# A new written order of steps for a fused attention and gated-FFN kernel, with eight reloaded weight chunks in place of six in block 2

## The chip, the cores and the metric

The kernel runs on one core of a Trainium2 chip. The metric is the device time of one execution in microseconds. The kernel before takes 946.95 us (median of 3 runs, 946.5 to 949.25).

## The reference

Linear attention over 8 batches, 8 heads, 576 positions and 64 values per head, then an RMS-normed, gated feed-forward network over the 4608 tokens that come out of it (model width 512, inner width 1536):

```python
q_s = np.exp(q - np.max(q, axis=-1, keepdims=True))
q_s = q_s / (np.sum(q_s, axis=-1, keepdims=True) + 1e-09)
k_s = np.exp(k - np.max(k, axis=2, keepdims=True))
k_s = k_s / (np.sum(k_s, axis=2, keepdims=True) + 1e-09)
kv = np.einsum('bhsd,bhse->bhde', k_s, v)
x = np.einsum('bhsd,bhde->bhse', q_s, kv)          # then reshaped to (4608, 512)
xn = x / np.sqrt(np.mean(x * x, axis=-1, keepdims=True) + 1e-06) * rms_g
g = xn @ w_gate
out = (g * (1.0 / (1.0 + np.exp(-g))) * (xn @ w_val)) @ w_out
```

Queries are softmaxed along the 64 values of a head, keys along the 576 positions; that is why the keys of a head group need a maximum over all positions before anything else can be done with them.

## The kernel before

**Tiling.** The 4608 tokens are nine blocks of 512. Blocks 0, 1 and 2 are computed plainly; the other six are taken as three pairs, whose two-block products are Strassen products (steps `pp` and, in the last two pairs, `qq` in place of the plain second product `f2p`). The inner width 1536 is twelve chunks of 128. A step number s = 12·j + i stands for chunk i of plain block j, so s = 0 to 11 is block 0, 12 to 23 block 1, 24 to 35 block 2. fp32 matmuls are three passes over halves in fp32r: each operand is split into a high half, a cast of it, and a low half, the operand less its high half.

**One chunk.** `f1.s.0` and `f1.s.1` (L964 to L974) are the gate and the value product of chunk s, twelve matmuls of 128x512 each, into one of only two PSUM banks of the pool `ps_gv`. `g_mul.s` (L977 to L979, DVE) reads the gate bank, `silu.s` (L982, ACT) works on the copy, and `h_mul.s` (L985, DVE) reads the value bank. So `f1.s+1.1`, which reuses the value bank, can't start ahead of the end of `h_mul.s`. `h_hi.s` and `h_lo.s` (L988 to L995) split the result, and `f2.s` (L998 to L1011) adds its product with the output weights to four banks, one chunk behind.

**Weights of a chunk.** Blocks 0 to 2 need gate, value and output weights of the chunk as halves. Each is either made anew on the engines from the weights held in SBUF (`w_hi`, L893, on ACT; `w_lo`, L896 to L898; `o_hi`, L901; `o_lo`, L904 to L906), or read back from the DRAM copy that `w_keep` and `o_keep` (L916 to L921, on SP's DMA queue) stored in block 1. `w_back` (L924 to L926, 1 MB) and `o_back` (L928 to L930, 512 KB) read back, issued from POOL. Both kinds of tile come from the pool `wsp` with two buffers, so that the halves of chunk s can be written only when chunk s−2 has been used for the last time. Before, chunks 24 to 29 make their halves and 30 to 35 read them back.

**Attention.** It is done by head groups, `b.n` being group n of batch b. `k_load` (L491 to L502, SP) brings the keys in, `k_max` (L533 to L535, DVE) takes the maximum of the parts, `k_tr` (L547 to L550, PE) transposes, `k_top` (L553, DVE) takes the maximum over positions, `k_rows` (PE), `k_sub` (DVE) and `k_exp` (ACT, table Exp) follow, then `k_mm` (L572 to L578, PE) makes the keys' product with the values. The steps `q_...` do the queries, ending with `q_x` (PE). A name with a 0 behind it, such as `k_max0`, is the form of it used for the first batch or batches. `warm` (L468 to L471) is a pair or a run of matmuls on a constant, whose result isn't used. `exp_table` (L473 to L476) is a small activation with Exp.

**What sets the order.** There is no planner in the kernel. One string, `ORDER` (lines 22 to 342, 3345 steps), lists the steps; each engine runs its own instructions in the order of the string, and DMAs go out in the order of the engine that issues them: loads, keeps and output stores on SP, reloads on POOL. A suffix puts a step on an engine (`:A` ACT, `:D` DVE, `:P` POOL):

```python
with tc.manual_schedule():
    for step in ORDER.split():
        step, _, engine = step.partition(":")
        name, *args = step.split(".")
        unit[0] = where[engine]
        steps[name](*map(int, args))
```

Of the kernel before, what the change touches and what calls it, by code (L numbers as in the profile page):

```python
# [27 lines left out]
q_eps0.0.1 k_top.0.2 q_exp.0.0 q_eps0.0.2 k_sub.0.1 v_load.0.2 k_tr.0.3 warm.2.13 conv_mul.0.1 k_rows.0.2 q_rec0.0.1  # L28
conv_low.0.1.1 q_rec0.0.2 warm.2.10 q_mul0.0.1:P k_sub.0.2 warm.2.3 k_exp.0.1 conv_shift.0.1 kv_zero.6 k_exp.0.2
q_t0.0.1 v_load.0.3 v_ones.1.0 q_mul0.0.2:P warm.2.12 k_top.0.3 k_eps.0.0 q_max0.0.3 conv_low.0.0.1 k_rows.0.3 warm.2.6  # L30
conv_add.0.1.1 k_rec.0.0 conv_mul.0.0 k_sub.0.3 q_t0.0.2 q_c0.0.1:A warm.2.4 g_load conv_shift.1.1 kv_norm0.0.0:A
k_mm.0.2 q_sub0.0.3:P load_w.0.2 k_exp.0.3 conv_shift.0.0 k_mm.0.1 k_load.1.0 k_eps.0.2 q_c0.0.2:A conv_add.0.0.1
# [5 lines left out]
conv_low.1.0.2 q_sub0.1.0:P load_w.1.2 q_x0.0.3 load_w.3.1 k_sub.1.0 load_w.2.1 n_sum0.1 x_hi.0.3:A o_hi.0:D x_lo.0.1
load_w.2.2 o_lo.0:P x_sq.0.3 n_sum0.2 v_load.1.0 conv_mul.1.0 x_lo.0.3 n_sum0.3 q_exp.1.0 conv_shift.1.0 warm.2.7
conv_add.1.0.2 conv_mul.2.0 n_t.0 warm.2.1 k_exp.1.0 f1.0.0.0.0 n_y0.0 f1.0.0.0.1 f1.0.0.0.2 q_max0.1.1 f1.0.0.0.3  # L40
f1.0.1.0.0 f1.0.0.1.0 conv_shift.2.0 load_w.4.0 f1.0.1.0.1 f1.0.1.0.2 q_sub0.1.1:P load_w.3.2 w_hi.1.0.2:A f1.0.1.0.3
n_y1.0 f1.0.0.1.1 load_w.3.0 f1.0.0.1.2 f1.0.0.1.3 q_load0.1.2 f1.0.1.1.0 q_exp.1.1 w_lo.1.1:P f1.0.1.1.1 f1.0.1.1.2
# [10 lines left out]
conv_add.3.2.1 conv_mul.5.1 f1.3.1 conv_mul.4.2 load_w.7.1 v_load.1.1 o_hi.2:A w_lo.3.0:P conv_shift.4.2 conv_low.5.0.2
o_lo.2:D conv_mul.5.0 f1.3.0 conv_add.4.0.2 conv_shift.5.1 o_hi.3:A conv_shift.5.0 h_hi.2:A conv_mul.6.1 q_sum0.1.2
load_w.7.2 load_w.6.2 q_eps0.1.2 w_hi.4.0.2:A load_w.8.1 h_lo.2:D k_tr.1.1 f2.2 load_w.8.0 g_mul.3 conv_low.4.2.1
w_lo.4.0:P k_top.1.1 q_rec0.1.2 silu.3 conv_shift.6.1 q_max.2.0 conv_add.5.0.2 k_rows.1.1 f1.4.0 conv_mul.5.2 k_sub.1.1
conv_low.5.2.1 h_mul.3 conv_mul.7.0 w_lo.4.1:P conv_shift.5.2 conv_low.6.0.2 f1.4.1 o_lo.3:P h_hi.3:A g_mul.4 k_max.1.2
silu.4 conv_add.4.2.1 k_exp.1.1 conv_shift.7.0 h_lo.3:P load_w.8.2 q_t0.1.1 load_w.10.1 k_tr.1.2 f2.3 q_c0.1.1:D
load_w.10.0 kv_zero.2 k_top.1.2 conv_add.5.2.1 conv_mul.7.1 q_half.2.0 w_hi.5.0.2:A conv_shift.7.1 kv_zero.5
load_w.10.2 o_hi.4:A w_lo.5.0:D v_load.1.2 k_mm.1.1 conv_low.7.0.2 o_lo.4:P k_rows.1.2 k_eps.1.1 f1.5.0 k_sub.1.2  # L60
q_max2.2.0 h_mul.4 q_sub.2.0:P q_max0.1.3 h_hi.4:A k_rec.1.1 conv_low.6.2.1 w_lo.5.1:D f1.5.1 q_exp.2.0 q_sub0.1.3:P
kv_norm0.1.1:D k_exp.1.2 g_mul.5 conv_add.6.0.2 q_sum.2.0 conv_mul.6.2 kv_hi.1.1:A q_half2.2.0 conv_low.7.2.1
conv_shift.6.2 q_x0.1.1 q_exp.1.3 h_lo.4:D f2.4 w_hi.6.0.2:A conv_add.7.0.2 x_hi.1.1:D x_sq.1.1 x_lo.1.1 silu.5
k_mm.1.2 w_lo.6.0:D load_w.9.1 conv_mul.8.0 f1.6.0 load_w.9.0 conv_add.6.2.1 k_eps.1.2 k_rec.1.2 o_hi.5:A q_sum0.1.3
h_mul.5 o_lo.5:P conv_shift.8.0 h_hi.5:A o_hi.6:A w_lo.6.1:D f1.6.1 conv_mul.8.1 g_mul.6 x_acc.1.1:P kv_norm0.1.2:A
w_hi.7.0.2:A kv_zero.3 q_eps0.1.3 h_lo.5:D conv_mul.8.2 w_lo.7.0:P q_rec0.1.3 conv_shift.8.1 f2.5 silu.6 q_sum2.2.0
conv_mul.7.2 o_lo.6:D conv_low.8.2.1 h_mul.6 q_mul0.1.2:P conv_shift.7.2 f1.7.0 q_rec.2.0 conv_add.7.2.1 conv_mul.9.1
conv_shift.8.2 kv_hi.1.2:A conv_low.8.0.2 w_lo.7.1:D v_ones.1.3 v_ones.2.1 load_w.9.2 v_load.2.1 conv_shift.9.1
conv_add.8.2.1 conv_low.10.2.1 q_t0.1.2 f1.7.1 q_c0.1.2:A conv_add.8.0.2 conv_mul.9.0 h_hi.6:A conv_shift.9.0
conv_low.9.0.2 g_mul.7 q_x0.1.2 h_lo.6:D silu.7 load_w.11.0 load_w.11.1 w_hi.8.0.2:A conv_add.9.0.2 f2.6 k_load.2.0  # L70
x_hi.1.2:D conv_mul.9.2 h_mul.7 x_sq.1.2 x_lo.1.2 o_hi.7:A load_w.11.2 conv_low.9.2.1 w_lo.8.0:D k_load.1.3 h_hi.7:A
f1.8.0 conv_shift.9.2 conv_mul.10.2 o_lo.7:D q_load.2.1 w_hi.9.0.2:A w_lo.8.1:D h_lo.7:D conv_mul.11.0 w_lo.9.1:P
# [1355 lines left out]
```

## Time and profile before

| what | value |
| --- | --- |
| median of 3 runs | 946.95 us (946.5 to 949.25) |
| the profiled execution | 947.29 us, its span 945.5 us |
| busy share of the span: PE, PEld, DVE, ACT, POOL | 98%, 79%, 77%, 50%, 57% |
| matmuls in the trace | 4625 |
| DMA | 211.79 MB, mean 224 GB/s |

PE is TensorE's matmuls, PEld its weight loads, DVE is VectorE, ACT ScalarE, POOL GpSimd, SP SyncE. Times in views are microseconds from the start of the span; L974 is line 974 of the kernel. A row of instructions has start, duration, engine, line, operation, tiles (written and read) and shapes; brackets hold the idle time ahead of it and what ended that. Four stretches help to find one's way: the first `f1` starts at 35.17, block 1's end lies near 268, the first paired product near 407, and the last matmul ends at 938.80.

### The profile page before, as it was taken

How to read it: one execution, taken by the hardware profiler on the slowest of the kernel's cores; microseconds unless marked ns; L12 is line 12 of the kernel's file. 1: busy time of each engine (PE TensorE's matmuls, PEld its weight loads, DVE VectorE, ACT ScalarE, POOL GpSimd, SP SyncE). 2: the span in 40 equal slices, each digit the busy share in tenths (PEclk: the TensorE clock that was granted, in tenths of full speed). 3: DMA queues.
4: the chain of work that ended last, by engine and by line, in shares of the span. 5: the costliest groups of instructions: out<-in, count | busy, mean ns of one | idle time of the engine just before them, and what ended most of it. 6: DMA issues, size and time to landing. Idle time of an engine off the chain costs nothing.

```text
span 945.5 us, 14391 instructions
## 1 busy us (share of the span) xinstructions
PE 922.8 (98%) x4625; PEld 747.9 (79%) x4625; DVE 728.3 (77%) x1522; ACT 468.9 (50%) x746; POOL 539.4 (57%) x531
## 2 busy tenths in 40 slices
...
GB/s 255 291 253 190 150 71 238 299 262 271 319 259 153 242 242 280 216 219 228 264 202 261 234 295 196 308 288 269 163 203 212 193 210 265 267 215 199 54 134 90
DMA packets 215463, 211.79 MB, mean 224 GB/s; under 512 B 139828, under 2 KB 176732, under 8 KB 210780
## 3 DMA queue, kind: packets, MB, share of 16 engines
...
## 4 chain that ended last, share of the span: by engine, by line
PE 78%; DMA 9%; DVE 6%; SPq 3%; ACT 1%; issue 1%; POOL 1%; DVEq 0%; POOLq 0%; ACTq 0%
PE ps_gv L1123 17%; PE ps_o L1123 12%; PE ps_gv L974 11%; PE ps_a L1123 7%; PE ps_o L1011 7%; PE ps_o L1332 6%; PE ps_o L1216 3%; PE ps_a L1332 3%; DMA qt<-in_q_dram 3%; PE ps_gv L1332 3%; PE ps_a L1216 2%; PE ps_gv L1216 2%; DMA kt<-in_k_dram 2%; PE ps_a L578 2%; DMA w<-in_moe_w_gate_dram 1%; PE ps_a L786 1%
## 5 line engine op out<-in xcount | busy, mean ns | idle before, releaser
L974 PE MATMUL ps_gv<-xh,w 128*128 128x512 f32 x576 | 190.3, 398 | 3.7 <-DVE gs L986 2.9
L1123 PE MATMUL ps_gv<-x,ring 128*128 128x512 f32 x576 | 143.0, 392 | 0.0
L974 PEld LDWEIGHTS ps_gv<-xh,w 128*128 128x128 f32 x576 | 108.8, 189 | 28.6 <-DVE gs L986 4.1
L1123 PEld LDWEIGHTS ps_gv<-x,ring 128*128 128x128 f32 x576 | 106.9, 188 | 22.3
L974 PE MATMUL ps_gv<-xl,w 128*128 128x512 f32 x288 | 112.5, 394 | 0.0
L1144 DVE TENSOR_TENSOR tmp<-tmp,ps_gv 128x512 f32<-128x512 f32 x84 | 57.2, 683 | 47.8 <-PE ps_gv L1123 46.2
L1123 PE MATMUL ps_o<-x,ring 128*128 128x512 f32 x360 | 85.0, 389 | 0.0
L1096 POOL DMA_DIRECT2D ring<-wd x54 | 30.9, 572 | 88.9 <-PE ps_gv L1123 39.8
L1123 PEld LDWEIGHTS ps_o<-x,ring 128*128 128x128 f32 x360 | 67.5, 188 | 14.3
L1011 PE MATMUL ps_o<-o,hh 128*128 128x512 f32 x288 | 74.3, 399 | 0.0
L974 PEld LDWEIGHTS ps_gv<-xl,w 128*128 128x128 f32 x288 | 54.7, 190 | 10.6 <-issue 0.2
L1011 PEld LDWEIGHTS ps_o<-o,hh 128*128 128x128 f32 x288 | 52.9, 188 | 12.2 <-issue 0.7
L409 ACT CAST hh<-gs 128x512 fp32r<-128x512 f32 x51 | 31.5, 617 | 49.4 <-POOL gs L1288 19.7
L898 POOL TENSOR_TENSOR w<-w,w 128x512 fp32r<-128x512 f32 x34 | 46.4, 1371 | 11.0 <-ACT w L409 4.3
L1144 DVE TENSOR_TENSOR tmp<-tmp,ps_o 128x512 f32<-128x512 f32 x42 | 28.7, 684 | 24.3 <-PE ps_o L1123 23.9
L535 DVE TENSOR_REDUCE cm<-kt 116x128 f32<-116x640 f32 x28 | 36.6, 1311 | 5.1 <-DMA kt<-in_k_dram 5.0
L1011 PE MATMUL ps_o<-o,hl 128*128 128x512 f32 x144 | 38.8, 391 | 0.9 <-DVE hl L995 0.9
L995 POOL TENSOR_TENSOR hl<-gs,hh 128x512 fp32r<-128x512 f32 x21 | 28.8, 1373 | 16.1 <-ACT hh L409 14.3
L1123 PE MATMUL ps_a<-x,ring 128*128 128x512 f32 x144 | 37.0, 392 | 0.0
L1123 PE MATMUL ps_a<-x,w 128*128 128x512 f32 x144 | 36.7, 390 | 0.0
L1096 POOL DMA_DIRECT2D w<-wd x18 | 10.2, 564 | 45.3 <-PE ps_a L1123 37.0
L1123 PE MATMUL ps_gv<-x,w 128*128 128x512 f32 x144 | 35.2, 392 | 0.0
...
## 6 DMA issues: line engine op xcount, KB each, us to landing
...
```

The source lines that it names most:

```text
L409: (e.copy if e is nc.scalar else e.tensor_copy)(dst, src)
L535: nc.vector.tensor_reduce(out=cm, in_=kt_[b, g].rearrange("p h j d -> p h d j"), axis=AX.X, op=ALU.max)
L578: nc.tensor.matmul(pk[h * D:(h + 1) * D, :D + 1], lhsT=ke[:n, h, j], rhs=vt[:n, j, h], start=(j == 0), stop=(j == len(rows) - 1))
L898: on(nc.gpsimd).tensor_tensor(out=w[:, :, 1], in0=halves(s % NF, a, 1)[:, 0], in1=w[:, :, 0].bitcast(F32), op=ALU.subtract)
L974: nc.tensor.matmul(pd[s], lhsT=w[:, a, c // 2, m, c % 2 * P:c % 2 * P + P], rhs=X[j, c][x], start=(n == 1), stop=(n == 3 * NKT))
L995: on(nc.gpsimd).tensor_tensor(out=hl, in0=g_[s], in1=h_[s][0].bitcast(F32), op=ALU.subtract)
L1011: nc.tensor.matmul(po[t], lhsT=a[:, t * P:(t + 1) * P], rhs=w, start=(i == 0 and n == 0), stop=(i == NF - 1 and n == len(terms) - 1))
L1096: nc.gpsimd.dma_start(t, src.rearrange("p a b f -> p (a b f)"))
L1123: nc.tensor.matmul(abc[p, i, m, b], lhsT=src[:, h, c * P:(c + 1) * P], rhs=operand(o, c, x), start=first and n == 0, stop=n == 5, skip_gro ...
L1144: nc.vector.tensor_tensor(out=dst, in0=ux[u + (src,)], in1=abc[u + (b,)], op=ALU.add)
L1216: nc.tensor.matmul(pa[p, t, k], lhsT=a[:, k * P:(k + 1) * P], rhs=w, start=(c == 0 and n == 0), stop=(c == NF - 1 and n == 2))
L1332: nc.tensor.matmul(qacc[p, b, x], lhsT=ws[l][x], rhs=h[m], start=first and i == 0 and n == 0, stop=i == NH - 1 and n == 2, skip_group_chec ...
```

## The change

Only the string `ORDER` changes; no function does. It has 3339 steps in place of 3345.

- Block 2 reads back chunks 28 to 35 in place of 30 to 35. Gone are `w_hi`, both `w_lo`, `o_hi` and `o_lo` of chunks 28 and 29; new are `w_back.28`, `w_back.29`, `o_back.28` and `o_back.29`. The DRAM copies they read are stored in block 1 as before.
- The first stage, up to the first `f1`, has another order: head groups of batch 0 finish in the order 0, 1, 3, 2; four `warm` pairs in place of two stand ahead of `k_tr.0.0`; `warm.2.9` moves there from the end of block 1; `exp_table` moves behind `silu.1`.
- The rest of blocks 0 to 2 has another order. PE's own steps change places mostly by a few positions, the small steps of DVE, ACT and POOL and the loads on SP by more. Some engine suffixes change (113 from DVE to POOL, 108 from POOL to DVE, 61 from ACT to DVE, 39 from DVE to ACT).
- From the second pair on PE's order is nearly the same. In the end two stores (`qput.2.11.1`) go behind those of `qput.2.21.1`.

The core of the diff, lines of the string:

```diff
@@ -20,325 +20,323 @@
 ORDER = """
-k_load.0.0 k_load.0.1 kv_zero.0 kv_zero.4 k_load.0.2 constants v_ones.0.3 q_load0.0.1 kv_zero.1 warm.2.11 v_ones.0.2
-v_ones.1.2 v_ones.0.1 v_ones.0.0 kv_zero0.0 q_load0.0.2 warm.2.8 k_max0.0.0 kv_zero0.1 k_load.0.3 k_max0.0.1 k_tr.0.0
-q_load0.0.0 warm.2.5 k_max0.0.2 warm.2.0 load_w.1.1 load_w.0.1 k_tr.0.1 v_load.0.0 k_top.0.0 q_max0.0.1 k_rows.0.0
-warm.9 q_max0.0.2 q_sub0.0.1:P k_sub.0.0 q_load0.0.3 q_sub0.0.2:P q_exp.0.1 q_max0.0.0 k_max0.0.3 load_w.0.0 v_load.0.1
-q_exp.0.2 q_sub0.0.0:P k_top.0.1 q_sum0.0.1 k_tr.0.2 k_exp.0.0 k_rows.0.1 warm.2.2 q_sum0.0.2 conv_mul.1.1 k_mm.0.0
...
-k_rec.0.2 q_sum0.0.0 q_exp.0.3 k_eps.0.1 kv_norm0.0.2:A k_rec.0.1 q_eps0.0.0 load_w.1.0 w_hi.0.0.2:A q_rec0.0.0
...
-q_mul0.1.0:P conv_mul.3.0 q_max0.1.2 w_hi.2.0.2:A load_w.5.0 h_lo.0:P conv_shift.3.0 q_t0.1.0 load_w.4.2 f2.0
-conv_mul.4.1 q_load.2.0 q_eps0.1.1 o_hi.1:A w_lo.2.1:P q_c0.1.0:D conv_low.3.0.2 g_mul.1 o_lo.1:D kv_hi.1.0:A
-conv_low.2.2.1 q_sub0.1.2:P conv_shift.4.1 q_x0.1.0 q_rec0.1.1 conv_mul.3.1 kv_zero.7 w_lo.2.0:D f1.2.0 conv_low.3.2.1
-v_ones.1.1 conv_shift.3.1 q_mul0.1.1:P silu.1 x_hi.1.0:A h_mul.1 conv_add.3.0.2 conv_mul.2.2 x_lo.1.0 x_sq.1.0 f1.2.1
-g_mul.2 conv_mul.3.2 conv_shift.2.2 h_hi.1:A load_w.5.2 w_hi.3.0.2:A h_lo.1:D load_w.7.0 conv_add.2.2.1 conv_shift.3.2
...
-h_hi.8:A conv_add.10.0.2 conv_mul.11.1 q_t0.1.3 f1.9.0 q_c0.1.3:D k_max.1.3 q_load.2.2 w_hi.10.0.2:A h_lo.8:D
-w_lo.10.1:P k_tr.1.3 f1.9.1 o_lo.8:D conv_add.9.2.1 k_top.1.3 g_mul.9 silu.9 k_rows.1.3 w_lo.10.0:D f1.10.0
...
-q_half.2.2 v_ones.2.0 v_load.2.0 q_load.2.3 w_lo.11.0:D f1.11.0 w_lo.11.1:P x_lo.1.3 x_acc.1.3:D q_max2.2.1 o_hi.11:D
...
-w_keep.22 q_load.4.0 q_lo.3.1:D o_lo.21:D q_x.3.0 h_mul.21 f1.22.0 s_add.4.1:D h_hi.21:A s_add.3.3:D w_hi.23.0.2:A
-h_lo.21:P s_hi.4.1:A o_hi.22:A q_sub.3.3:P q_x.3.1 g_mul.22 f1.22.1 k_max.3.3 o_lo.22:P silu.22 s_keep.1.3 x_sq.3.1
-o_keep.21 k_max.4.0 x_sq.3.0 s_hi.3.3:A q_exp.3.3 q_rec.3.2 w_lo.23.0:D f2.21 s_lo.4.1:D x_acc.3.1:D s_keep.4.1
-w_hi.24.0.2:A s_add.3.4:D v_load.3.3 w_lo.23.1:D s_hi.3.4:A f1.23.0 q_sum.3.3 s_add.5.3:P o_hi.23:A h_mul.22
...
-h_hi.25:A f1.26.1 g_mul.26 o_lo.25:P kv_hi.4.0:A k_max.4.1 silu.26 h_lo.25:P q_sum2.4.1 q_rec.4.1 kv_lo.4.0 k_load.4.2
...
-k_max.4.2 silu.27 k_load.4.3 v_ones.4.3 s_lo.4.4:P q_half2.4.2 v_load.4.3 n_lo.3:P k_eps.4.1 k_rec.4.1 q_t.4.1
-kv_hi.4.1:A f2.26 w_lo.28.0:P h_mul.27 x_sq.4.0 kv_lo.4.1 q_hi.4.1:A s_lo.5.4:D o_hi.27:A h_hi.27:A q_sum2.4.2
...
-n_t.3 q_mul.4.2:P q_exp.4.3 h_lo.27:D q_lo.4.1:P n_y0.3 s_hi.5.3:A k_rows.4.2 f1.28.1 k_sub.4.2 s_keep.4.4 o_lo.27:P
-q_t.4.2 r_keep.3 k_exp.4.2 q_sum.4.3 q_load.5.0 w_lo.29.0:P q_half2.4.3 q_x.4.1 g_mul.28 w_back.30 f2.27 x_sq.4.1
-k_max.4.3 s_lo.5.3:P x_cp.4.1:A silu.28 n_y1.3 w_lo.29.1:P s_keep.5.3 k_tr.4.3 f1.29.0 q_sum2.4.3 q_rec.4.3 h_mul.28
...
-x_nm.3.1:D v_ones.5.0 x_nm.3.3:D b_hi.0.0.1:A o_in.0.0.0 k_rec.4.3 v_load.5.0 k_max.5.0 b_lo.0.0.1:P kv_hi.4.3:A
...
-qb_lo.2.4.3:D qput.2.11.1 qpua.2.11.1 qb_hi.2.4.4:A qb_hi.2.4.5:D qput.2.22.1 qq.2.4.3 qb_hi.2.3.0:A qb_lo.2.4.4:D
...
-qb_lo.2.3.4:D qput.2.21.0 qpua.2.21.0 qb_hi.2.3.5:D qput.2.21.1 qpua.2.21.1 qq.2.3.3 qb_lo.2.3.5:P qq.2.3.4.0
...
+k_load.0.0 k_load.0.1 kv_zero0.0 k_load.0.2 constants v_ones.0.0 q_load0.0.1 v_ones.1.1 warm.2.1 v_ones.0.3 v_ones.0.2
+kv_zero.4 kv_zero.5 v_ones.0.1 q_load0.0.2 kv_zero0.1 warm.2.2 k_max0.0.0 k_load.0.3 warm.2.8 q_load0.0.0 warm.2.3
+load_w.1.1 load_w.0.1 k_tr.0.0 warm.2.10 k_top.0.0 v_load.0.0 k_max0.0.1 k_rows.0.0 warm.2.6 q_max0.0.1 k_tr.0.1
+q_load0.0.3 k_sub.0.0 q_sub0.0.1:P load_w.0.0 k_exp.0.0 kv_zero.1 k_max0.0.2 v_load.0.1 k_top.0.1 k_tr.0.2 k_max0.0.3
+q_exp.0.1 q_sum0.0.1 k_tr.0.3 v_load.0.2 warm.2.13 k_top.0.2 q_max0.0.0 k_rows.0.1 conv_low.0.1.1 q_eps0.0.1 k_top.0.3
...
+f1.0.0.2.3 f1.0.1.2.0 w_lo.1.0:P conv_mul.1.2 f1.0.1.2.1 conv_shift.2.1 f1.0.1.2.2 conv_low.1.2.1 f1.0.1.2.3 g_mul.0
+conv_mul.4.1 conv_add.2.0.2 q_sum0.1.1 f1.1.0 silu.0 load_w.5.1 conv_shift.4.1 k_load.1.1 conv_shift.1.2 conv_mul.4.0
+q_eps0.1.1 h_mul.0 conv_add.1.2.1 w_hi.2.0.2:A load_w.6.0 k_mm.1.0 conv_shift.4.0 load_w.6.1 w_lo.1.1:P f1.1.1
+conv_low.3.0.2 k_eps.1.0 k_rec.1.0 g_mul.1 load_w.5.0 q_rec0.1.1 conv_mul.3.0 kv_norm0.1.0:D kv_zero.3 kv_zero.7
+h_hi.0:A q_mul0.1.1:D load_w.4.2 conv_low.2.2.1 conv_shift.3.0 w_lo.2.1:P q_t0.1.0 silu.1 q_max0.1.2 conv_mul.3.1
+h_lo.0:D f2.0 q_load.2.0 q_c0.1.0:A conv_shift.3.1 q_sub0.1.2:P kv_hi.1.0:A conv_mul.2.2 exp_table w_lo.2.0:D q_exp.1.2
...
+w_hi.10.0.2:A h_lo.8:D conv_add.9.2.1 conv_shift.11.0 q_x0.1.2 w_lo.10.1:P k_tr.1.3 o_hi.9:A f1.9.1 k_top.1.3 q_max.2.1
+x_hi.1.2:A g_mul.9 w_lo.10.0:P x_lo.1.2 silu.9 q_mul.2.0:P k_rows.1.3 f1.10.0 k_sub.1.3 o_lo.8:P k_max.2.0 k_exp.1.3
+q_half.2.1 q_t0.1.3 q_t.2.0 x_sq.1.2 f2.8 o_lo.9:D q_c0.1.3:A conv_mul.11.1 x_acc.1.2:D conv_mul.11.2 conv_shift.11.1
...
+k_eps.2.0 q_rec.2.1 o_hi.13:A k_load.2.2 s_add.2.1:P k_rec.2.0 q_sum.2.2 k_exp.2.1 q_half2.2.2 kv_hi.2.0:A o_lo.13:P
...
+s_keep.0.1 v_load.2.2 store.0.3:A store.0.2:A w_hi.14.0.2:A f2.12 s_lo.1.2:D s_hi.1.1:A s_add.1.4:D x_hi.2.0:A
...
+h_mul.21 s_keep.3.4 x_sq.3.0 q_mul.3.1:D w_keep.22 o_hi.21:A q_half2.3.3 h_hi.21:A o_lo.21:P f1.22.1 q_t.3.1 h_lo.21:D
+q_hi.3.1:A o_keep.21 k_load.4.0 q_sum2.3.3 s_hi.2.3:A g_mul.22 q_lo.3.1:P s_hi.5.1:A q_rec.3.3 f2.21 o_hi.22:A
+q_mul.3.3:D w_lo.23.0:P q_t.3.3 q_load.4.0 q_hi.3.3:A w_lo.23.1:D silu.22 q_x.3.1 q_t.3.2 s_lo.2.3:P f1.23.0 h_mul.22
+x_sq.3.1 o_lo.22:D s_hi.4.3:A h_hi.22:A k_max.3.3 s_lo.5.1:P f1.23.1 s_keep.2.3 g_mul.23 s_keep.5.1 q_lo.3.3:D silu.23
...
+kv_hi.4.0:A h_hi.25:A w_lo.27.1:P k_rows.4.1 g_mul.26 f1.26.1 q_sum2.4.1 v_load.4.2 silu.26 q_rec.4.1 h_lo.25:P
...
+n_sum.3 g_mul.27 v_load.4.3 f1.27.1 h_lo.26:P k_rec.4.1 q_rec.4.2 kv_hi.4.1:A n_t.3 silu.27 kv_lo.4.1 o_lo.26:D q_t.4.1
+q_x.4.0 w_back.29 k_max.4.2 f2.26 s_add.5.3:P x_sq.4.0 q_load.5.0 x_cp.4.0:A h_mul.27 q_mul.4.2:P s_hi.5.3:A n_y0.3
...
+o_lo.27:P s_keep.5.2 q_half2.4.3 s_keep.5.3 q_load.5.1 k_top.4.2 h_lo.27:P g_mul.28 q_sum2.4.3 k_max.4.3 silu.28
...
+k_top.4.3 x_nm.3.3:P h_mul.28 k_rows.4.3 f1.29.0 q_t.4.3 h_hi.28:A x_nm.3.1:P k_sub.4.3 x_sq.4.1 q_load.5.2 n_cols.2
...
+q21.2.1 qput.2.21.0 qpua.2.21.0 qtr.2.21.1 qq.2.3.2 qb_hi.2.3.5:D qput.2.21.1 qpua.2.21.1 qb_lo.2.3.4:D qb_lo.2.3.5:D
+qput.2.11.1 qq.2.3.3 qq.2.3.4.0 qq.2.3.5.0 qq.2.3.4.1 q12.2.0 qq.2.3.5.1 qtr.2.12.0 q12.2.1 qput.2.12.0 qpua.2.12.0
...
```

More of the change, by code (lines that the diff above doesn't have):

```diff
@@ L28 @@
[L28 to L32, printed above, removed]
@@ L38 @@
[L38 to L42, printed above, removed]
@@ L53 @@
[L53 to L72, printed above, removed]
```

552 lines of the change are left out of this document (290 added, 262 removed).

## The prediction

> **What bounds the kernel now.** I first read the profile cut into stages: lead-in, the plain blocks 0, 1 and 2, the passage to the paired blocks, those blocks, and the tail. Columns: stretch, length, busy time of PE, PEld, DVE, ACT, POOL, clock, DMA share, GB/s.
>
> ```profile
> 0.00:35.17 35.17, 27.21 (x178) 17.64 (x179) 26.86 (x63) 22.59 (x40) 21.17 (x40) 1.00 1.06 273
> 35.17:145.00 109.83, 108.03 (x547) 86.69 (x545) 95.82 (x176) 84.49 (x126) 86.42 (x69) 1.00 0.62 173
> 145.00:268.00 123.00, 117.78 (x638) 94.62 (x639) 102.66 (x250) 80.26 (x125) 92.42 (x81) 0.99 0.88 285
> 268.00:407.00 139.00, 137.94 (x782) 112.78 (x781) 118.95 (x309) 98.39 (x153) 110.63 (x110) 1.00 0.89 230
> 407.00:583.00 176.00, 176.00 (x930) 144.43 (x929) 148.27 (x350) 87.63 (x142) 96.51 (x107) 1.00 0.87 242
> 583.00:938.80 355.80, 355.80 (x1557) 291.71 (x1555) 234.29 (x376) 95.50 (x163) 132.23 (x129) 1.00 0.68 205
> 938.80:945.50 6.70, 0.00 (x1) 0.00 (x0) 1.44 (x3) 0.00 (x0) 0.00 (x0) 0.77 0.57 78
> ```
>
> From 407 to 938.8 us PE does nothing but work. What an order of steps can still give lies ahead of 407: 7.96 us idle in the lead-in (35.17 − 27.21), 1.80 in block 0, 5.22 in block 1, 1.06 in block 2, and matmuls at a lower clock. The view of PE's waits from 35.17 to 410 names them (waiting tile and line, releaser, total, times, longest):
>
> ```profile
> PE ps_gv L974 <- DVE gs L986: 2.9, 3, 2.3
> PE ps_a L836 <- DVE kt L566: 1.1, 1, 1.1
> PE ps_a L578 <- DMA qt<-in_q_dram: 0.9, 1, 0.9
> PE ps_o L1011 <- DVE hl L995: 0.9, 1, 0.9
> PE ps_a L550 <- DVE w L461: 0.8, 1, 0.8
> ...
> PE ps_a L550 <- DVE cm L535: 0.3, 1, 0.3
> ```
>
> The longest one, 2.3 us, ends at 259.81. Around it stand these two stretches, and in the chain of waits the matmul groups that follow:
>
> ```profile
> 257.56:259.81 2.25, 0.00 (x0) 0.00 (x0) 2.22 (x5) 0.62 (x1) 1.77 (x2) 0.99 1.03 391
> 259.81:264.40 4.59, 4.59 (x13) 3.69 (x14) 4.42 (x14) 2.41 (x5) 3.38 (x3) 0.63 0.80 230
> ```
>
> ```profile
> 259.81 4.59 PE ps_gv L974 x12
> 264.40 2.72 PE ps_o L1011 x12
> ```
>
> After 2.25 us without work the clock falls to 0.63, and twelve matmuls take 4.59 us where twelve take 2.72: the stall costs 2.25 + 1.87 = 4.12 us.
>
> [...]
>
> **Why it stalls.** DVE's timeline (start, duration, engine, line, tiles) over the stall:
>
> ```profile
> 249.37 0.68 DVE L979 TENSOR_TENSOR gs<-ps_gv,r 128x512 f32<-128x512 f32 x1
> 252.94 2.52 DVE L535 TENSOR_REDUCE cm<-kt 116x128 f32<-116x640 f32 x2 [2.89 <-DMA kt<-in_k_dram]
> 255.39 0.23 DVE L757 RECIPROCAL sm<-sm 128x16 f32<-128x16 f32 x1
> 255.54 0.62 DVE L898 TENSOR_TENSOR w<-w,w 128x512 fp32r<-128x512 f32 x1
> ...
> 259.08 0.68 DVE L986 TENSOR_TENSOR gs<-ps_gv,gs 128x512 f32<-128x512 f32 x1
> ```
>
> The first row is g_mul.22, the last h_mul.22, which frees the bank that f1.23.1 writes. Between them stand k_max.3.3 and k_max.4.0 (2.52 together) and seven small steps. PE's work from the end of f1.22.0 to f1.23.1 is three groups of 2.72 and some 0.75 of small products, 8.9 us; DVE's own work is 8.2 (the rows' starts, less the wait). DVE had 0.7 us to spare and waited 2.89 for keys: 2.2 late. The keys were late at their issue, in SP's queue, which issues them one behind the other:
>
> ```profile
> 246.02 2.46 SPq L499 DMA_DIRECT2D kt<-in_k_dram  x2
> 248.53 1.08 SPq L500 DMA_DIRECT2D kt<-in_k_dram  x1
> ```
>
> **The change part by part.**
>
> *Chunk 22.* In the new order five short steps stand between g_mul.22 and h_mul.22 (four at 0.6 to 0.8, one reciprocal at 0.23, 4.1 us with the two ends); k_max.3.3 and k_max.4.0 stand behind h_mul.22. Spare time grows from 0.7 to 4.8 us, and no load is in it. −2.25 − 1.87 = −4.1. What is late next: k_max.3.3 then delays k_tr.3.3, which stands a chunk later, behind f2.22.
>
> *Transposes of key maxima.* For seven head groups the old order lets PE come to k_tr while DVE is still at its k_max; in the new one at least 1.4 us of other matmuls stand there. The rows of L550 (0.8 and 0.3) are waits of that kind. I take −0.5 between −1.1 (both gone) and 0 (moved elsewhere).
>
> *Two more reloaded chunks.* Removed: for s = 28 and 29 two w_hi and two o_hi on ACT, five of the low-half subtractions on POOL, one on DVE. Added: four DMAs from POOL, 3 MB. Rows of before for the reloads (issue on POOL; its waits; landing) and for the subtraction they replace:
>
> ```profile
> L926 POOL DMA_DIRECT2D w<-wd x6: 706/762/892, 313.0 to 361.8; - x6
> ...
> DMA to landing us min/median/max: 6.0/6.9/8.5
> ```
>
> ```profile
> L898 POOL TENSOR_TENSOR w<-w,w 128x512 fp32r<-128x512 f32 x34 | 46.4, 1371 | 11.0 <-ACT w L409 4.3 <-DMA vt<-in_v_dram 2.9 <-DVE w L409 1.9
> ```
>
> ```profile
> 287.69 5.44 PE ps_gv L974 x24
> 306.70 2.77 PE ps_gv L974 x12
> ```
>
> The buffer of w_back.28 is free after f1.26.1 (287.69 + 5.44 = 293.13) and needed at f1.28.0 (306.70): 13.6 us for a landing of 6.0 to 8.5. POOL's w_lo.27.1 and h_lo.25 ahead of it take 1.37 each, which leaves 2.4 us at worst; w_back.29 is placed one chunk later with the same distance, and o_back moves half the bytes. POOL gains five times 1.37 less four issues of at most 0.89, but POOL (110.63 of 139) bounds nothing here: PE idles 1.06 us in the whole stage. So 0, at best −1.06; with the cover gone, each us of delay is a us of PE. Queue: w_back.30 now stands behind o_back.28 in POOL's order; the 0.5 MB go ahead of 1 MB that had a chunk's time in hand.
>
> *First stage.* Its rows on PE:
>
> ```profile
> 2.21 2.07 PE L471 MATMUL ps_gv<-mean_w 128*128 128x512 f32 x4 [2.21 <-POOL mean_w L432]
> ...
> 33.84 1.49 PE L471 MATMUL ps_gv<-mean_w 128*128 128x512 f32 x4
> 35.17 1.09 PE L974 MATMUL ps_gv<-xh,w 128*128 128x512 f32 x4
> ```
>
> SP's order of loads is the same up to q_load0.1.2, so what arrives first is unchanged. [...] Head groups run 0, 1, 3, 2, and the last, q_x0.0.2, ends where q_x0.0.3 did, to within a us, followed by the same four n_sum0. warm.2.9 is moved here from the end of block 1: two matmuls, 2 × 2.72/12 = 0.45, which make f1.0 later by as much as block 1 gets shorter; that cancels. For the rest: of the 7.96 us idle, 2.21 precede the first matmul and stay; a quarter of the other 5.75 won is −1.5, one wait for late data as long as the longest above is +2.9. I take +0.5, near the middle, since the chains are redrawn and not shortened.
>
> *Tables on ACT.* By the order of Exp and Silu on ACT, table loads rise from 50 to 56, five of the six in blocks 0 and 1:
>
> ```profile
> 67.62 1.28 ACT L983 ACT_TABLE_LOAD   x1
> 68.92 0.63 ACT L983 ACTIVATE gs<-gs 128x512 f32<-128x512 f32 x1
> ```
>
> The activation starts 0.02 us behind the load, so 1.28 each, 7.7 together. ACT is busy 84.49 of 109.83 and 80.26 of 123.00: I take 0, and as upper bound all six on the path, +7.7.
>
> [...]
>
> *Tail.* The two stores of qput.2.11.1 go behind those of qput.2.21.1 on SP, an issue of about 1.1 each by the SP row above, long before the last matmul at 938.80; what they can delay is the last store of the 6.70 us. I take +0.2, between 0 and half an issue, 0.6.
>
> *New tight places.* Elsewhere the new order changes nearly all positions but no amounts: the same 4625 matmuls, in blocks 0 and 1 DVE 422 steps for 424, POOL 145 for 148. Places are redrawn, so new short waits replace old; I take 0 and give the bounds to the rivals.
>
> **Sum:** the profiled execution ran 947.29 us (span 945.50 and 1.79 around it): 947.3 − 4.1 − 0.5 + 0.5 + 0 + 0.2 = 943.4. The median, 946.95, is 0.34 lower: 943.1, say 943.2.
>
> **The rivals.**
>
> *Stall redrawn.* Five waits of 0.3 to 1.1 us stood beside the big one before; block 1 is as full as it was (DVE 102.66 of 123). A wait of some 2 us with its slow clock comes back at another chunk: 943.2 + 4.1 = 947.3. For it: where DVE holds a key maximum between g_mul and h_mul the spare time is small. Against it: by the same count as for chunk 22, the least spare time from chunk 14 to 34 is now 2.7 us (chunk 33), where the old order has 0.7 and 1.5. v_load.3.1 now goes ahead of k_load.3.2 on SP's queue, but its k_max.3.2, between g_mul.19 and h_mul.19, has 4.5 to spare, more than 2.89.
>
> *Slower: keys late in block 0.* The new order puts k_max.1.1 between g_mul.1 and h_mul.1, k_max.2.0 into chunk 9 and k_max.2.2 into chunk 13. With 0.6 for a 128x512 step and 1.25 for a maximum, DVE has 7.8, 8.0 and 7.7 us to do there, PE 9.2, 9.6 and 9.2: spare 1.4, 1.6 and 1.5. k_load.1.1 is issued 6.1 us of PE's work ahead of its use where it had 17.9. The rows on waits for keys and on the old h_mul.1, which had no maximum ahead of it:
>
> ```profile
> DVE cm L535 <- DMA kt<-in_k_dram: 5.0, 3, 2.9
> ```
>
> ```profile
> 53.23 0.69 DVE L986 TENSOR_TENSOR gs<-ps_gv,gs 128x512 f32<-128x512 f32 x1 [0.41 <-ACT gs L983]
> ```
>
> If each of the three waits 2.9 us as k_max.3.3 did, PE stalls 1.5 + 1.3 + 1.4 = 4.2 and runs three groups at the lower clock, 5.6: 943.2 + 9.8 = 953.0. It decides from a wait of about 1.4 us on; one such place alone gives back 3.3. For it: the cut lead of k_load.1.1. Against: k_load.2.0 keeps 20 us of lead and k_load.2.2 6.5 (5.7 before), and block 0 moves 173 GB/s where the stage with the late keys moved 285.
>
> *Slower: table loads on the path.* 943.2 + 7.7 = 950.9, if each of the six sits between g_mul and h_mul with no time to spare.
>
> *The reload isn't hidden.* Two landings at 8.5 behind a busy POOL, 2 us late each, with the clock's 1.87: 943.2 + 7.7 = 950.9 too. The 13.6 us speak against it.
>
> **How the numbers follow.** Forecast 0.46, stall redrawn 0.30, late keys 0.15, table loads 0.05, reload not hidden 0.04. Runs of this kernel lie within about 0.3%, 2.8 us, so faster means under 944.1 and slower over 949.8. The forecast's own range, 939.5 (idle of block 2, lead-in and transposes all won: −1.06, −2.0, −0.6 against the sum) to 944.1, is faster: 0.46. The redrawn stall is within: 0.30. The last three are slower: 0.24. The range leaves out the upper half of the late keys and the corner below 938.8: 938.8 to 952.
>
> **What would show it.** Right: PE's wait for gs from L986 near 257 us gone, no stretch of clock below 0.9 between 40 and 400, f1.0 starting within a us of 35.2, no PE wait ended by a reload. Wrong: a new wait over 2 us on L974 in blocks 0 or 1 (with kt from the key input ahead of it on DVE it is the third case), a first f1 after 37.7, or a DMA w<-wd releasing PE near 300 to 320.

## The result and the profile after

The changed kernel takes 956.65 us (median of 6 runs, 951.56 to 959.03) beside 946.81 us for the kernel before on the same chips (6 runs); the ratio is 1.0101 (95% interval 1.0084 to 1.0117). The forecast was 943.2, between 938.8 and 952, with 46% for faster; the kernel became slower, and the time lies outside that range. The profiled execution took 955.77 us, its span is 954.0.

Lines of the changed kernel's code stand two lower than before (L984 is h_mul, L972 f1, L646 the query load, L548 k_tr); in the kernels of the experiments they move by a few lines, and the tiles in a row tell the step. PE's waits from 35.17 to 410 us after, first rows:

```profile
PE ps_gv L972 <- DVE gs L984: 6.8, 3, 5.9
PE ps_a L576 <- ACT sq L801: 2.1, 1, 2.1
PE ps_a L834 <- DVE kt L564: 1.4, 1, 1.4
```

The longest is a wait for h_mul again, but not the one of before. Stretches of the profile after (same columns as in the prediction):

```profile
0.00:35.20 35.20, 29.06 (x182) 19.96 (x183) 27.21 (x65) 22.68 (x39) 20.09 (x38) 0.90 1.06 278
35.20:145.00 109.80, 109.52 (x555) 88.15 (x554) 96.49 (x180) 86.89 (x127) 89.51 (x73) 1.00 0.59 168
145.00:268.00 123.00, 118.91 (x653) 95.42 (x652) 109.02 (x250) 83.28 (x131) 88.12 (x76) 1.00 0.90 295
268.00:327.00 59.00, 56.78 (x339) 46.22 (x338) 45.79 (x132) 45.22 (x71) 50.81 (x49) 0.97 0.87 242
327.00:337.00 10.00, 4.06 (x14) 2.96 (x13) 4.08 (x14) 2.44 (x3) 3.03 (x4) 0.73 0.86 189
```

Block 0 is nearly free of idle time now (0.28 us for 1.80). Block 2, which had 1.06 us of idle time in 139, has 5.94 us in these ten microseconds, at a clock of 0.73. PE's and DVE's rows there:

```profile
334.55 0.80 PE L972 MATMUL ps_gv<-xh,w 128*128 128x512 f32 x1 [5.94 <-DVE gs L984]
```

```profile
332.13 0.69 DVE L712 TENSOR_REDUCE st<-qt 128x16 f32<-128x512 f32 x1 [7.92 <-DMA qt<-in_q_dram]
...
333.81 0.68 DVE L984 TENSOR_TENSOR gs<-ps_gv,gs 128x512 f32<-128x512 f32 x1
```

DVE stands for 7.92 us at q_max.5.1, which the order puts between g_mul.29 and h_mul.29, and waits for its queries; f1.30.1 waits for h_mul.29. The queries are late on SP's queue. SP's rows for the first two query loads of block 5 before, and for all three after (8 DMAs each):

```profile
306.16 4.75 SPq L648 DMA_DIRECT2D qt<-in_q_dram  x8
...
312.48 5.32 SPq L648 DMA_DIRECT2D qt<-in_q_dram  x8
```

```profile
305.46 7.51 SPq L646 DMA_DIRECT2D qt<-in_q_dram  x8
...
314.41 18.85 SPq L646 DMA_DIRECT2D qt<-in_q_dram  x16
```

Eight issues took 4.75 and 5.32 us before, and 3.88 for the third load; they take 7.51 after, and the sixteen of the last row 9.45 and 6.91 with a pause of 2.48 between them. POOL's row for the second of the new reloads stands just ahead of them:

```profile
302.51 0.77 POOL L924 DMA_DIRECT2D w<-wd  x1 [1.34 <-PE ps_gv L972]
```

Where the profiled executions stand at the seams of the stages (us; start of the step, or its end where that is said; from the steps' own instructions in each trace; E1, E2 and E9 are the kernels e1_six, e2_eight and e9_block0 below):

| step | before | after | E1 | E2 | E9 |
| --- | --- | --- | --- | --- | --- |
| f1.0 | 35.17 | 34.96 | 35.56 | 35.78 | 35.17 |
| f1.12.0 | 145.36 | 142.47 | 143.13 | 144.74 | 142.87 |
| f1.24.0 | 267.87 | 262.87 | 263.50 | 267.32 | 266.09 |
| end of f2.35 | 405.74 | 411.32 | 406.45 | 415.06 | 404.32 |
| pp.1 | 582.95 | 591.35 | 588.37 | 592.26 | 582.98 |
| end of the last matmul | 938.80 | 947.36 | 943.36 | 948.06 | 939.22 |

The end of f2.35 is the end of block 2; the first paired product starts ahead of it, at 378.80 before. After runs 5.0 us ahead at f1.24.0 (2.9 up to f1.12.0, 2.1 more from block 1), loses 10.6 us in block 2 and 2.8 more up to the second pair. Not all of that stands near 328: f2.26 ends at 305.43 after, 305.97 in E1 and 306.13 before, so most of the lead is gone in both kernels of the new order before a query of block 5 can be late.

### The profile page after: what moved, and what is told of

It is laid out like the page before. It is cut to its first block, busy times and chain, and to the rows that moved or that the text cites. A ratio compares the mean times of both kernels' runs of the same rounds, so it can differ in the third digit from the quotient of the medians.

```text
span 954.0 us, 14390 instructions
## 1 busy us (share of the span) xinstructions
PE 926.0 (97%) x4625; PEld 751.0 (79%) x4625; DVE 735.8 (77%) x1537; ACT 461.1 (48%) x727; POOL 547.1 (57%) x535
## 5 line engine op out<-in xcount | busy, mean ns | idle before, releaser
L972 PE MATMUL ps_gv<-xh,w 128*128 128x512 f32 x576 | 192.3, 401 | 7.9 <-DVE gs L984 6.8
L972 PEld LDWEIGHTS ps_gv<-xh,w 128*128 128x128 f32 x576 | 109.3, 190 | 34.6 <-DVE gs L984 8.0
L972 PE MATMUL ps_gv<-xl,w 128*128 128x512 f32 x288 | 113.1, 396 | 0.0
L972 PEld LDWEIGHTS ps_gv<-xl,w 128*128 128x128 f32 x288 | 55.1, 191 | 10.8 <-issue 0.4
L407 ACT CAST hh<-gs 128x512 fp32r<-128x512 f32 x43 | 26.6, 618 | 40.7 <-DVE gs L984 19.3
L993 POOL TENSOR_TENSOR hl<-gs,hh 128x512 fp32r<-128x512 f32 x23 | 31.0, 1347 | 15.4 <-ACT hh L407 8.0
L712 DVE TENSOR_REDUCE st<-qt 128x16 f32<-128x512 f32 x28 | 19.0, 679 | 20.5 <-DMA qt<-in_q_dram 19.6
```

The costliest lines, as they stand in the source:

```text
L407: (e.copy if e is nc.scalar else e.tensor_copy)(dst, src)
L712: nc.vector.tensor_reduce(out=st[:, :, 0], in_=qt_[j, g], axis=AX.X, op=ALU.max)
L972: nc.tensor.matmul(pd[s], lhsT=w[:, a, c // 2, m, c % 2 * P:c % 2 * P + P], rhs=X[j, c][x], start=(n == 1), stop=(n == 3 * NKT))
L993: on(nc.gpsimd).tensor_tensor(out=hl, in0=g_[s], in1=h_[s][0].bitcast(F32), op=ALU.subtract)
```

## The experiments

Theory T1: the two added reloads delay other loads. Rival T2: the new places of the loads and steps in the order do it, and the reload has no part.

**Eight reloads in the old order, six in the new.**

```diff
 e2_eight, the order before
-w_hi.28.0.2:A w_lo.28.0:P w_lo.28.1:D o_hi.28:A o_lo.28:P (and the same five of chunk 29)
+w_back.28 (behind f2.25)  w_back.29 (behind s_keep.5.4)  o_back.28 (ahead of w_back.30)  o_back.29 (behind n_rows.3)
 e1_six, the new order
-w_back.28 w_back.29 o_back.28 o_back.29
+the ten steps again; b_hi.0.3.1, which writes over weights they read, behind f1.30.0
```

> The kernel before with eight chunks read back, and nothing else of the change. T1: the query loads issued from 306 to 326 us take longer to issue and to land, DVE waits for queries between g_mul.29 and h_mul.29, where the old order has about 5 us to spare; 947 to 952, with DMA busy over nine tenths from 293 to 330. T2: the old places of the loads hide it, 946 to 947.5, and no new PE wait over 1 us.

> The new order, but chunks 28 and 29 make their halves on the engines as the kernel before does, and six chunks are read back. Theory T1 (traffic): the 3 MB more on the DMA engines make q_load.5.1 land late, and DVE meets it as q_max.5.1 between g_mul.29 and h_mul.29. Without them PE's wait for gs near 328 us falls from 5.9 to under 1 us, its slow clock (about 2 us) goes too, and the time is about 956.7 - 8 = 948.7. Theory T2 (place in the queue): q_load.5.1 is late because SP issues it about 8 us later than before, behind two stores, and the reload has no part in it: the wait stays at 4 us or more and the time at 955 to 957.

Measured: e2_eight 958.77 us, ratio 1.0114 (1.0078 to 1.0151), which is more than T1 named; e1_six 950.53, ratio 1.0032 (1.0013 to 1.0052). The reload alone, in the old order, costs as much as the whole change. PE loses it at another place there: DVE's waits for queries between g_mul.29 and h_mul.29 (4.0 us) find the spare time that T1 gave them, but h_lo.29 stands on DVE behind q_max.5.2, which waits 3.7 us more for its queries, and PE waits 4.2 us for h_lo.29 at f2.29. Taken out of the new order, the reload gives back 0.69% (1.0101 to 1.0032), 6.5 us, and PE's wait near 328 is gone. What is left is 0.32%, to which the last two sections come back. T2 falls for the greater part.

**The bytes without the reload.** Copies that nobody waits for, beside an otherwise untouched kernel:

```diff
 e8_idle, the kernel before
+def w_idle(s):   # 1 MB, as w_back reads it, into a DRAM tile wx that nobody reads
+    ...
+    nc.gpsimd.dma_start(wx[:, :, at:at + 2]..., parts_of(i, at, 2))
+def o_idle(s):   # 512 KB
+    nc.gpsimd.dma_start(ox, od[s % NF])
+steps w_idle.28, w_idle.29, o_idle.28, o_idle.29 at e2_eight's places
 e12_idle_early: four such copies of 3.1 MB of q together, behind f2.4, f2.5, f2.6 and f2.7
```

> The kernel before, whole, plus four copies DRAM to DRAM from POOL's queue (2 x 1 MB and 2 x 512 KB) where the eight-chunk kernel has w_back.28, w_back.29, o_back.28 and o_back.29; nobody waits for them and the halves are still made on the engines. Theory T1 (traffic): the bytes alone delay the loads behind them, about what eight reloads cost in this order, 953 to 958, with DVE waiting 3 us or more for queries between 320 and 340. Rival T3 (the reloaded tiles themselves: their buffers, waits on POOL and PE): the idle copies cost under 2 us, 946 to 949.

> The kernel before plus four idle copies DRAM to DRAM of 3.1 MB together on POOL's queue in block 0, behind f2.4 to f2.7 (about 85 to 120 us), where the DMA engines are busy some 0.6 of the time. Traffic theory: bytes cost where the DMA engines are full and little where they are not, so 947 to 949. If the cost of such copies is their issue on POOL or their bytes as such, it is as with the idle copies near 300 us, 956 to 960.

Measured: e8_idle 959.13, ratio 1.0123 (1.0068 to 1.0178), a little over T1's 958; e12_idle_early 945.81, ratio 0.9985 (0.9968 to 1.0003). The bytes alone cost what the reload costs, with all halves still made on the engines and no tile waiting for them; the same amount in block 0 costs nothing that can be measured. So it isn't the reloaded tiles (T3), nor the issue on POOL, nor bytes as such; it is what else is to be loaded while they move. One difference stays: a copy writes to DRAM what a reload writes to SBUF, and no run separates the two.

**Which of the bytes.**

```diff
 e11_seven, the order before: chunk 29 read back, chunk 28 made (w_back.29 and o_back.29 as in e2_eight)
 e13_idle_280, the kernel before
+w_idle.29 behind f1.26.0, o_idle.29 behind f1.26.1
 e14_idle_w303
+w_idle.29 behind s_keep.5.4
 e15_idle_o318
+o_idle.29 behind n_rows.3
```

> The kernel before with seven chunks read back (29 to 35): half of the 3 MB more. By traffic: between nothing (the first megabytes go into idle DMA time near 285 to 310 us) and half of the 11.5 us that eight cost in this order, 947 to 953. If a single place decides (chunk 28's reload), it is 946.5 to 948.

> The kernel before plus one idle copy of 1 MB and one of 512 KB from POOL behind f1.26.0 and f1.26.1, about 285 to 291 us, where the DMA engines are 0.4 busy and no query load of block 5 is issued yet. If only a full stretch costs, 947 to 948.5. If 1.5 MB anywhere in block 2 pushes back what comes behind it, it is as with seven reloads, 954 to 957.

> The kernel before plus the 1 MB idle copy alone, where seven reloads have w_back.29 (about 303 us, DMA engines 0.55 busy until 309, the query loads of block 5 issued from 306 on). If the slow issue of the query DMAs behind a large copy is what counts, most of the 9.5 us of seven reloads is here, 951 to 956. If only the fuller stretch from 317 on counts, 947 to 949.

> The kernel before plus the 512 KB idle copy alone, where seven reloads have o_back.29 (about 318 us, DMA engines 0.94 busy and more until 340). If the full stretch is what counts, it costs about 0.5 MB at some 300 GB/s, 1.7 us, and up to the clock's 2 us on top, 948.5 to 951. If the query loads' issue at 306 to 313 counts, nothing: 946.5 to 947.5.

Measured: e11_seven 956.39, ratio 1.0097 (1.0070 to 1.0125); e13_idle_280 949.27 beside 948.35, ratio 1.0033 (1.0009 to 1.0056); e14_idle_w303 955.40, ratio 1.0081 (1.0056 to 1.0105); e15_idle_o318 948.28, ratio 1.0005 (0.9992 to 1.0018). Half of the 3 MB costs nearly all, more than the 953 us that e11's traffic theory allowed, and within it the 1 MB near 303 us, although the DMA engines are far from full there before (0.47 busy from 301 to 306, 0.57 from 306 to 311). The 512 KB near 318, where they are full (0.94 busy from 317 to 325 before, 1.07 from 325 to 333), cost nothing that can be measured in the median, and 1.5 MB near 285 cost 0.3%, between what e13's two theories named. SP's and POOL's rows of e14:

```profile
303.00 0.89 POOL L939 DMA_DIRECT2D wx<-wd  x1
```

```profile
304.84 7.20 SPq L648 DMA_DIRECT2D qt<-in_q_dram  x8
...
313.60 7.52 SPq L648 DMA_DIRECT2D qt<-in_q_dram  x8
```

and of e13, whose copies are over by then:

```profile
307.49 4.72 SPq L648 DMA_DIRECT2D qt<-in_q_dram  x8
...
313.77 5.26 SPq L648 DMA_DIRECT2D qt<-in_q_dram  x8
```

4.72 and 5.26 us as before; 7.20 beside the copy, and 7.52 for the next load, although the copy had landed by then (7.5 us after its issue). What PE loses in e14 comes later, at f2.29, whose h_lo.29 stands behind q_max.5.2 on DVE. DVE's row for q_max.5.2 and PE's for f2.29, and PE's for f2.29 in e15:

```profile
335.86 0.69 DVE L714 TENSOR_REDUCE st<-qt 128x16 f32<-128x512 f32 x1 [4.55 <-DMA qt<-in_q_dram]
...
339.96 2.07 PE L1022 MATMUL ps_o<-o,hl 128*128 128x512 f32 x4 [5.37 <-DVE hl L1006]
```

```profile
339.25 2.08 PE L1022 MATMUL ps_o<-o,hl 128*128 128x512 f32 x4 [4.74 <-DVE hl L1006]
```

The same place in these kernels of the old order (us, from each trace):

| run | its three query loads of block 5, to issue | DVE starts q_max.5.2 | PE waits at f2.29 | ratio |
| --- | --- | --- | --- | --- |
| before | 4.75, 5.32, 3.88 | 330.74 | no | 1 |
| e13_idle_280 | 4.72, 5.26, 4.24 | 333.06 | 1.1 | 1.0033 |
| e14_idle_w303 | 7.20, 7.52, 5.93 | 335.86 | 5.4 | 1.0081 |
| e11_seven | 6.43, 7.99, 6.62 | 337.33 | 3.0 | 1.0097 |
| e2_eight | 5.53, 8.33, 7.59 | 338.78 | 4.2 | 1.0114 |
| e8_idle | 5.02, 5.94, 5.54 | 340.61 | 4.1 | 1.0123 |
| e15_idle_o318 | 4.84, 5.19, 4.79 | 335.15 | 4.7 | 1.0005 |

The later q_max.5.2 can start, the longer the kernel takes (single traces beside medians), and that fits better than the length of the query loads' own issue. In e8 the first two of these are issued nearly as fast as before, but begin 4.4 and 4.7 us later: its trace is 1.3 us later ahead of the copies already, and the keys ahead of the queries, issued around the end of the first copy, take from 302.17 to 306.08 where they took from 300.52 to 301.97. So in e8 and e14 what SP issued beside a copy or soon behind it came later, queries or not. e15 is the row that doesn't fit. Its profiled execution took 951.81, the longest of its ten (median 948.28), and has the wait of the others. A copy near 318 can thus meet the same wait, and the median says only that it mostly doesn't; how often can't be told from one trace.

In the view of SP's own waits from 295 to 335 us, e14 has rows in which a query load (L648) waits for older transfers of other tiles on SP's queue:

```profile
SPq L648 <- DMA kt<-in_k_dram: 2.1, 2, 1.7
SPq L648 <- DMA wd<-parts: 2.0, 2, 1.1
```

Before, no query load waits so there, but a key and a value load (L499, L524) do, for queries:

```profile
SPq L499 <- DMA qt<-in_q_dram: 1.9, 1, 1.9
...
SPq L524 <- DMA qt<-in_q_dram: 0.6, 1, 0.6
```

A query load needs nothing of the keys or the parts, so I read these rows thus: in e14 SP's queue held query loads back until older transfers on it were done (2.1 and 2.0 us in the rows above), and eight issues took 7.20 us beside the 1 MB copy from POOL's queue, for 4.75 without it. The times are shown. That the copy slowed those older transfers, and that everything behind in SP's order came later for that, is my inference; no run shows it.

**Can the order hide the late queries?** First their reader is moved, then their issue:

```diff
 e3_qmax, the new kernel
-q_max.5.1 v_ones.5.1 q_rec.5.0 q_half.5.1 kv_hi.4.3:A f1.30.0 o_back.30 q_max2.5.1 h_mul.29
+v_ones.5.1 q_rec.5.0 kv_hi.4.3:A f1.30.0 o_back.30 h_mul.29 q_max.5.1 q_half.5.1 q_max2.5.1
 e7_qfirst, the new kernel
 v_load.4.3, s_keep.5.2 and s_keep.5.3 moved behind q_load.5.1
```

> The new kernel with q_max.5.1, q_half.5.1 and q_max2.5.1 moved behind h_mul.29 on DVE; loads, reloads and their order are untouched. If the price comes from a late load that DVE meets at that place (both T1 and T2), DVE still waits for queries until about 332 us, but h_mul.29 is done near 325 and PE loses under 2 us there: 948 to 951. If the DMA traffic itself slowed PE (late weights or a lower clock), the time stays at 955 to 957.

> The new kernel with v_load.4.3, s_keep.5.2 and s_keep.5.3 moved behind q_load.5.1 on SP's queue, so that the queries of block 5 are issued up to 8 us earlier; the same bytes. If only the place of the late load costs, the 5.9 us wait near 328 us goes to under 1.5 and the time falls by about 7, to 949 to 951. If the DMA engines have no room there (T1 in its strict form), another load (v_load.4.3, k_load.5.0 or q_load.5.2) is late in its place and the time stays above 953.

Measured: e3_qmax 955.05, ratio 1.0075 (1.0045 to 1.0104), a gain of 0.26% on 1.0101 that the intervals don't separate from none; e7_qfirst 958.75, ratio 1.0105 (1.0068 to 1.0142), no gain. In both the same loss stands one step on, at k_tr.5.0 (L548). e3's and e7's rows in the view of PE's waits:

```profile
PE ps_a L548 <- DVE cm L533: 6.3, 1, 6.3
```

```profile
PE ps_a L548 <- DVE cm L533: 6.0, 1, 6.0
```

k_max.5.0, on which k_tr.5.0 waits, stands on DVE behind q_max.5.2, the third of them, and DVE waits there for 5.93 us in e3 and 7.90 in e7; q_max.5.1 itself waits 0.70 and 0.17. Both expectations of a gain of 6 to 8 us fall: the queue as a whole is late, not one load, and moving one reader or one load passes the wait on.

**The old stall by itself.**

```diff
 e4_ch22, the kernel before
-g_mul.22 f1.22.1 k_max.3.3 ... k_max.4.0 ... h_mul.22
+g_mul.22 f1.22.1 ... h_mul.22 k_max.3.3 k_max.4.0
```

> The kernel before with only k_max.3.3 and k_max.4.0 moved behind h_mul.22 on DVE. Forecast's step: the 2.25 us wait near 257 us and its 1.87 us of slow clock go, 946.8 - 4.1 = 942.7. Rival (stall redrawn): DVE's wait for the keys shifts the steps behind it, and a like stall shows at f1.24 or k_tr.3.3: 946 to 947.

Measured: 947.83, ratio 1.0003 (0.9981 to 1.0024), near the rival's time. The wait near 257 is gone, and a like one stands 3 us later, at f2.22 and not where the rival looked for it. e4's PE row and chain of waits:

```profile
263.86 2.38 PE L1010 MATMUL ps_o<-o,hh 128*128 128x512 f32 x5 [2.87 <-ACT hh L408]
```

```profile
250.44 5.63 DMA wd<-w
...
257.06 5.51 DMA od<-o
...
262.67 0.62 ACT o L408
263.29 0.53 ACT hh L408
```

f2.22 waits for h_hi.22; ahead of it on ACT stands o_hi.23, which waits until 262.67 for the store o_keep.21 to have read its buffer. The store is late on the same SP queue. The forecast's 4.1 us were the price of the longest wait, not what its removal brings.

**First part and rest.** After 630 steps both orders have done the same set of steps, so they can be joined there.

```diff
 e9_block0: the new order's steps 1 to 630, then the order before from step 631
 e10_rest: the other way about (eight reloads)
```

> The new order for the first 630 steps (first stage and block 0, up to k_tr.2.0; both orders have done the same set of steps there), the order of the kernel before for the rest, six reloads. In the traces the new order reaches f1.12.0 2.9 us earlier. If PE's waits set the end, the time is 947 - 2.9 = 944. If the loads of blocks 1 and 2 set the pace (DMA engines about 0.9 busy from 145 to 400 us), the head start is given back: 946.5 to 948.

> The opposite: the first 630 steps of the kernel before, the rest of the new order with eight reloads. If the new first part brings 2.9 us, this is 956.7 + 2.9 = 959.5; if a head start is given back, it is as the new kernel, 956 to 957.5.

Measured: e9_block0 944.83 beside 946.85 (12 and 23 runs), ratio 0.9987 (0.9971 to 1.0003); e10_rest 959.48, ratio 1.0110 (1.0067 to 1.0153). The first part brings at most 0.3% and may bring nothing. e10's four runs lie between 950.4 and 962.7, which doesn't separate its two expectations; 1.0110 beside the 1.0101 of the change would be 0.09% for the first part. In e9's trace (of an execution of 947.73, longer than its median) the lead is 2.5 us at f1.12.0, 1.4 at the end of f2.35 and nothing at pp.1. PE's 2.3 us wait of before stands in it unchanged, near 255 us:

```profile
PE ps_gv L973 <- DVE gs L985: 2.3, 1, 2.3
```

e9_block0 is the only kernel here whose median lies 2 us under the kernel before, but its interval holds 1, so none is shown to beat it.

**Two that settle less.**

```diff
 e6_six_keep: e1_six with w_keep.23 ahead of s_keep.2.3
 e5_splice: the new order to f1.24.0 (with that w_keep.23), then what is left in the order before
```

> The new order with six reloads, and w_keep.23 moved ahead of s_keep.2.3 on SP's queue. In the new order w_hi.25 waits on ACT until 268.7 us for the store of w_keep.23 out of the same buffer, and PE then waits 2.1 us for x_sq.3.2 behind it. Theory: an earlier store lets w_hi.25 start about 1.5 us earlier and the stall near 272 us goes or halves: 950.5 less 2 to 4, 946.5 to 948.5. Rival: the store lands no earlier since the DMA engines are full there (0.9 busy): 950 to 951.

> The new order up to f1.24.0 (with w_keep.23 ahead of s_keep.2.3), and from there the steps that are left in the order of the kernel before, with six reloads. In the new kernel's trace f2.23 ends 5.1 us earlier than before. If that gain is real and block 2 is where the loss is, the time is 946.8 - 5 = about 942. If the earlier arrival only moves PE up to loads that come no sooner, the gain is given back within block 2 and the time is 946 to 948.

Measured: e6_six_keep 950.65, ratio 1.0034 (1.0014 to 1.0055), as e1_six; its wait for x_sq is 1.8 us in place of 2.1. e5_splice 950.76, ratio 1.0040 (1.0015 to 1.0064). The orders don't match at f1.24.0: at the seam a dozen steps left over from the old order come at once, and its trace has new PE waits of 2.8 and 2.4 us there. It says nothing certain on whether the lead of 5 us could be kept; e9_block0 is the cleaner joint.

## Why the prediction was wrong, step by step

- **Chunk 22, −4.1.** In the new kernel the wait is gone: its view by windows has 2.25 us busy at clock 1.00 where 2.25 idle and a clock of 0.63 followed before.

```profile
257.56:259.81 2.25, 2.25 (x12) 1.86 (x11) 2.25 (x5) 1.45 (x3) 0.23 (x1) 1.00 1.00 264
259.81:264.40 4.59, 4.59 (x25) 3.70 (x24) 4.26 (x8) 3.00 (x5) 2.73 (x2) 1.00 0.55 156
```

  But block 1 became only 2.1 us shorter, and e4_ch22 shows why −4.1 was too much in the old order: "what is late next" was looked for on DVE (k_tr.3.3), and it was a store on SP's queue with ACT waiting behind it. What took up the rest in the new order was not looked for. One reading is off by its own rule: by the rows' starts DVE's work is 7.5 us (249.37 to 259.76, less 2.89); 8.2 is about the sum of the rows' lengths, which overlap.
- **Transposes, −0.5.** At k_tr PE waited 0.78 and 0.34 us before (in blocks 0 and 1) and waits 0.97 after (in block 1), so these waits mostly moved elsewhere, the term's other bound. Block 0 all the same became 2.7 us shorter from f1.0 to f1.12.0, its idle time fell from 1.80 to 0.28. Before's rows, the second of them f2.4, the third warm.2.9:

```profile
66.05 0.32 PE L550 MATMUL ps_a<-ident,cm 116*128 116x116 f32 x1 [0.78 <-DVE w L461]
...
88.37 1.20 PE L1011 MATMUL ps_o<-o,hl 128*128 128x512 f32 x4 [0.85 <-DVE hl L995]
...
143.65 0.62 PE L471 MATMUL ps_gv<-mean_w 128*128 128x512 f32 x2
```

  The two waits are gone. warm.2.9 ran at the end of block 0, not of block 1 as the texts ahead have it, so 0.46 us of the 2.7 only changed place. By e9_block0 little or none of the gain reaches the end of the kernel.
- **Two more reloaded chunks, 0, at best −1.06.** This step failed. The reloads themselves land in time (no PE wait is ended by w<-wd; 6.0 to 9.8 us to landing), as forecast. Its text set "13.6 us for a landing of 6.0 to 8.5" against each other, and the queue it looked at was POOL's. It left out SP's queue, whose query loads are issued while w_back.29 is under way and after it. In the new kernel they took 7.51, 9.45 and 6.91 us to issue, in e1_six 4.75, 4.81 and 3.84; DVE waits 7.92 us for them ahead of h_mul.29, and PE 5.94 behind that. The two reloads cost 1.14% (10.8 us) in the old order and 0.69% (6.5 us) in the new.
- **First stage, +0.5.** f1.0 starts at 34.96 for 35.17: 0.2 us earlier, though warm.2.9 now stands ahead of it.
- **Tables, 0.** The view by lines has 56 loads, as counted from the order; one of 1.28 us stands on ACT ahead of the x_sq for which PE waits 2.1 us near 272. What the six add was not tested alone.
- **Tail, +0.2.** The last matmul ends 6.64 us ahead of the span's end, for 6.70.
- **New tight places, 0.** With six reloads the new order is still 0.32% slower (e1_six), so this term was wrong too. In its trace block 2 takes 142.95 us from f1.24.0 to the end of f2.35, for 137.87, and the stretch to pp.1 181.92 for 177.21. Its two longest PE waits stand there:

```profile
PE ps_a L577 <- ACT sq L802: 2.1, 1, 2.1
...
PE ps_gv L1122 <- DVE tmp L1143: 2.5, 1, 2.5
```

  The first has w_hi.25 ahead of it on ACT, but an earlier store did not cure the time (e6_six_keep). What makes these stretches longer is open.
- **The rivals.** Late keys in block 0 (0.15): did not come, no PE wait over 0.25 us in that block. Stall redrawn (0.30): came true for the step by itself (e4_ch22), but as a part of a loss. Table loads on the path (0.05): not tested. The reload isn't hidden (0.04) named the right part of the change, and its price of 7.7 us lies between the 6.5 and 10.8 measured, but that is luck: it expected weights that land late, and what came late was queries. Its point of decision, 13.6 us against the landing, is not what decides.
- **The signs named.** "A stretch of clock below 0.9" and a new wait over 2 us came, in block 2 and not in 0 or 1; a DMA w<-wd releasing PE did not.

Parts in per cent of the kernel before: first 630 steps −0.13 (e9_block0), the rest of the new order +0.45 (e1_six less e9_block0), the two reloads +0.69, together +1.01, by the way they are taken. All three rest on ratios whose intervals are 0.3 to 0.4 wide, and the reloads' part depends on the order (1.14 in the old one).
